# A sliding-window attention and gated MLP kernel on one core: from scheduled and woven tiles to one hand-written order

## The chip, the cores and the metric

The kernel runs on one core of a Trainium2 chip. Times are device microseconds (us) of the whole program. Every ratio uses runs in the normal ("fast") state of the program, on the same chip and in the same rounds as runs of the kernel before; differences in us between two variants can be between sessions. The engines are PE (matmul; PEld is its weight load), DVE (vector), ACT (scalar), POOL (general purpose) and SP (which here only issues DMA). Each engine works off its own queue of instructions in order, and waits for the others where it needs their results.

Words used below: **T** is a tile of 512 tokens (nine of them); **s1** is the first matmul of the MLP for a tile (64 matmuls of 512 columns, in 16 blocks of 4), **s2** the second (another 64). A **bank** is a piece of PSUM of 512 float32 a partition, into which PE writes; both kernels use eight. **Stage 0** is the stretch from s1 of tile 0 to the start of s1 of tile 1.

## The reference

```python
def _attn_ref(q, k, v):                    # q, k, v: [8, 8, 576, 64] float32
    scores = (1 / sqrt(64)) * q @ k^T      # per batch and head
    mask: 0 <= i - j < 64                  # causal, window of 64
    attn = softmax(where(mask, scores, -1e9))
    return attn @ v

def reference(...):
    x = attn_out.transpose(0, 2, 1, 3).reshape(4608, 512)
    h = x @ w_in                           # [512, 2048]
    g = h * clip(h + 3, 0, 6) / 6
    return g @ w_out                       # [2048, 512] -> [4608, 512]
```

## The kernel before

A scheduler (the framework's) reorders instructions. The program text weaves s1 of tile T with s2 of tile T-1, and both with the attention of batch T+1:

```python
    for T in range(NTB):
        side = []
        if T + 1 < B:
            nb = Batch(T + 1)
            if T + 1 < NPE:                           # NPE = 2: batches 0 and 1
                for h0 in (0, 4):
                    nb.cast_qk(pend, 0, h0, 4, pcopy)     # q on POOL
                    nb.cast_qk(pend, 1, h0, 4, vcopy)     # k on DVE
                    ...
            else:
                nb.by_dma(pend)                       # casts, then DMA transposes of q and k
            ...
            side = attention(nb)
        main = zipped(s1(T), s2(T - 1) if T else None)
        weave(main, 32 if T else 16, side, (0.6, 0.5)[T] if T < 2 else 0.0)
```

s1 has two banks (`ps_h`, "hT"), the scores four, the value product one ("o"), s2 one ("acc"). A block of s1 holds its bank until ACT and DVE are done with it:

```python
        for fc in range(NFC):                         # 16 blocks
            hT = ps_h.tile([P, TB], F32, name="hT")
            for g in range(NG):                       # 4 matmuls of 512 columns
                nc.tensor.matmul(hT[:], lhsT=win16[:, g, fc * P : (fc + 1) * P],
                    rhs=xT[:, g, t0 : t0 + TB], start=(g == 0), stop=(g == NG - 1))
            t1 = t1pool.tile([P, TB], BF16, name="t1")
            nc.scalar.activation(out=t1[:], in_=hT[:], func=RELU, bias=half[:], scale=1.0 / 6.0)
            nc.vector.scalar_tensor_tensor(out=gT[:, fc, :], in0=t1[:], scalar=1.0, in1=hT[:], op0=MIN, op1=MULT)
            yield
```

The attention output `opg` (tokens on partitions) must be transposed into `xT`. For batches 0 and 1 PE does it (`xt_pe`), for the others a DMA (`xt_dma`):

```python
    def xt_dma(bt, g):
        opg = opgs.pop((bt.b, g))
        nc.sync.dma_start_transpose(
            out=xT[:, g, bt.b * S : bt.b * S + SP].rearrange("d (k s) -> d k s", s=P),
            in_=opg[:].rearrange("p k h d -> p (k h d)"))
```

The results of s2 leave through two SBUF buffers (`osb`): ACT copies a bank into one of them, and SP issues the store.

The softmax here doesn't subtract the row's maximum and nothing guards it: scores larger than these inputs give would overflow.

## Time and profile before

Times: 374.21 us, median of 3 runs (372.58 to 378.02).

| stretch of the span | what goes on | PE busy of 10 us |
|---|---|---|
| 20 to 50 us | end of batch 0, first loads of w_in | 2.7, 1.9, 6.4 |
| 70 to 90 us | batch 1, first matmuls of s2 | 5.2, 8.4, at a clock of 0.64 and 0.51 |
| 120 to 130 us | batch 2's x, first use of transposes by DMA | 5.9, at a clock of 0.70 |
| 140 us to the end | middle stages and end | 217 of 231 us |

From the page of the kernel before: the span and the busy time of each engine with its share, and, from the span in 40 equal slices, the busy tenths of PE, the granted PE clock in tenths and the busy tenths of the DMA engines.

```profile
span 371.4 us, 5615 instructions
PE 314.0 (85%) x2124; PEld 155.2 (42%) x2160; DVE 187.5 (50%) x342; ACT 183.5 (49%) x293; POOL 71.4 (19%) x104
...
PE   1730499669998699989998997999999999999985
...
PEclk9999999956999699999999999999999999999999
DMA  7999999999119997999899899995112300110111
```

A slice is 9.3 us. From the fifteenth on PE is busy nearly all the time. Before that there are holes, and after two of them the clock is low, so that work in those slices takes up to twice as long. The same from the table by stretches (stretch, its length, busy us and number of instructions of each engine, granted clock, DMA share, GB/s):

```profile
20.00:30.00 10.00, 2.73 (x32) 1.89 (x30) 1.84 (x3) 2.60 (x5) 3.99 (x7) 1.00 1.20 234
30.00:40.00 10.00, 1.89 (x23) 1.57 (x23) 3.64 (x8) 0.64 (x1) 0.99 (x1) 1.00 1.18 246
40.00:50.00 10.00, 6.38 (x47) 4.14 (x49) 3.54 (x10) 2.17 (x4) 4.04 (x5) 1.00 1.14 219
70.00:80.00 10.00, 5.17 (x50) 3.22 (x50) 7.15 (x13) 3.53 (x6) 2.44 (x2) 0.64 0.98 198
80.00:90.00 10.00, 8.40 (x45) 4.26 (x47) 2.75 (x6) 2.66 (x4) 4.02 (x8) 0.51 1.00 192
120.00:130.00 10.00, 5.88 (x30) 2.10 (x31) 1.33 (x2) 2.48 (x5) 1.03 (x2) 0.70 1.15 228
```

A clock of 1.00 is not shown for 20 to 50 us: the clock record of this trace begins at 48.91 us, and a stretch without a record counts as 1.00.

The table of waits gives, for PE, who waited for whom (us in total, times, longest). Three of its lines:

```profile
PE hT L335 <- DVE opg L319: 11.8, 3, 10.6
PE hT L379 <- DMA xT<-opg: 9.2, 6, 2.7
...
PE acc L395 <- ACT osb L402: 3.0, 4, 0.9
```

The longest single wait is 10.6 us on DVE. The timeline (start, duration, engine, line, what it writes and reads, idle time before it and what ended it) shows why DVE was late:

```profile
34.18 0.69 DVE L227 CAST kn<-kst 128x1024 bf16<-128x1024 f32 x1 [8.92 <-DMA kst<-in_k_dram]
34.79 1.15 DVE L292 TENSOR_TENSOR pT_139<-pT_139,mask 128x1920 bf16<-128x1920 bf16 x1
35.86 0.19 DVE L316 RECIPROCAL rec<-o 128x5 f32<-128x5 f32 x1
36.08 0.49 DVE L319 TENSOR_TENSOR opg<-o,rec 128x320 bf16<-128x320 f32 x1
...
36.63 0.50 PE L335 MATMUL hT<-ident,opg 128*128 128x128 bf16 x3 [10.64 <-DVE opg L319]
...
47.16 1.06 PE L379 MATMUL hT<-xT,win_154 128*128 128x512 bf16 x2 [0.22 <-issue]
```

A cast for **batch 1** stood in DVE's queue before batch 0's last mask and normalisation, and waited 8.9 us for a load. PE stood behind it, and the first matmul with w_in came at 47.16 us.

### The profile page before, as it was taken

How to read it: one execution, taken by the hardware profiler on the slowest of the kernel's cores; microseconds unless marked ns; L12 is line 12 of the kernel's file. 1: busy time of each engine (PE TensorE's matmuls, PEld its weight loads, DVE VectorE, ACT ScalarE, POOL GpSimd, SP SyncE). 2: the span in 40 equal slices, each digit the busy share in tenths (PEclk: the TensorE clock that was granted, in tenths of full speed). 3: DMA queues.
4: the chain of work that ended last, by engine and by line, in shares of the span. 5: the costliest groups of instructions: out<-in, count | busy, mean ns of one | idle time of the engine just before them, and what ended most of it. 6: DMA issues, size and time to landing. Idle time of an engine off the chain costs nothing.

```text
span 371.4 us, 5615 instructions
## 1 busy us (share of the span) xinstructions
PE 314.0 (85%) x2124; PEld 155.2 (42%) x2160; DVE 187.5 (50%) x342; ACT 183.5 (49%) x293; POOL 71.4 (19%) x104
## 2 busy tenths in 40 slices
PE   1730499669998699989998997999999999999985
PEld 1520344343444244544544453445444444444432
DVE  6622446842477165646646662766476443433300
ACT  1540158713585266476646564664756354544411
POOL 4523224405200152044204402330000000000000
PEclk9999999956999699999999999999999999999999
DMA  7999999999119997999899899995112300110111
GB/s 225 214 231 239 229 208 194 202 188 193 51 35 180 230 212 122 189 233 213 160 209 221 154 183 210 217 191 116 48 46 49 92 30 28 51 36 29 56 56 58
DMA packets 155867, 54.12 MB, mean 146 GB/s; under 512 B 144064, under 2 KB 150208, under 8 KB 155840
## 3 DMA queue, kind: packets, MB, share of 16 engines
q1 hardware_dynamic: 152640, 49.56, 68.0%
q0 software_dynamic: 3200, 4.19, 6.4%
q8 instruction: 17, 0.28, 0.3%
q14 instruction: 10, 0.08, 0.1%
HBM read 36.70 MB, written 9.44 MB: 124 GB/s over the span
## 4 chain that ended last, share of the span: by engine, by line
PE 69%; DMA 10%; SPq 9%; DVE 5%; ACT 4%; issue 2%; another core or an unknown queue 1%; ACTq 0%; DVEq 0%
PE hT L379 31%; PE acc L395 30%; DMA xT<-opg 6%; SPq L80 4%; DMA kst<-in_k_dram 4%; PE st L276 3%; SPq L105 3%; PE o L305 2%; PE o L310 2%; DVE gT L385 1%; DVE opg L319 1%; SPq L218 1%; DVE pT_136 L292 1%; SPq L111 1%
## 5 line engine op out<-in xcount | busy, mean ns | idle before, releaser
L379 PE MATMUL hT<-xT,win_154 128*128 128x512 bf16 x560 | 151.7, 386 | 13.9 <-DMA xT<-opg 9.2
L395 PE MATMUL acc<-wout_155,gT 128*128 128x512 bf16 x556 | 147.3, 385 | 4.2 <-ACT osb L402 3.0
L379 PEld LDWEIGHTS <-win_154 128*128 128x128 bf16 x576 | 54.9, 99 | 71.0 <-issue 13.5
L395 PEld LDWEIGHTS <-gT 128*128 128x128 bf16 x576 | 53.4, 99 | 67.9 <-issue 10.8
L217 POOL CAST qn<-qst 128x512 bf16<-128x512 f32 (+1 forms) x30 | 19.0, 675 | 104.9 <-DMA qst<-in_q_dram 97.5
L319 DVE TENSOR_TENSOR opg<-o,rec 128x320 bf16<-128x320 f32 x64 | 31.4, 491 | 2.0
L402 ACT COPY osb<-acc 128x512 f32<-128x512 f32 x36 | 21.1, 587 | 20.8 <-PE acc L395 16.9
L316 DVE RECIPROCAL rec<-o 128x5 f32<-128x5 f32 x64 | 12.3, 192 | 27.8 <-PE o L310 27.8
L217 POOL CAST kn<-kst 128x512 bf16<-128x512 f32 (+1 forms) x30 | 17.1, 612 | 19.3 <-DMA kst<-in_k_dram 17.9
L204 POOL CAST V_142<-vst 64x512 bf16<-64x512 f32 (+2 forms) x11 | 11.7, 1082 | 20.4 <-DMA vst<-in_v_dram 16.5
L284 ACT ACTIVATE pT_130<-st 128x768 bf16<-128x768 f32 x16 | 12.2, 810 | 6.8 <-PE st L276 6.8
L292 DVE TENSOR_TENSOR pT_130<-pT_130,mask 128x1920 bf16<-128x1920 bf16 x8 | 10.5, 1312 | 8.0 <-ACT pT_130 L289 8.0
L284 ACT ACTIVATE pT_139<-st 128x768 bf16<-128x768 f32 x16 | 12.1, 807 | 4.4 <-PE st L276 4.2
L292 DVE TENSOR_TENSOR pT_136<-pT_136,mask 128x1920 bf16<-128x1920 bf16 x8 | 10.8, 1349 | 5.5 <-ACT pT_136 L289 5.5
L284 ACT ACTIVATE pT_136<-st 128x768 bf16<-128x768 f32 x16 | 12.0, 807 | 2.2 <-PE st L276 2.2
L284 ACT ACTIVATE pT_133<-st 128x768 bf16<-128x768 f32 x16 | 12.1, 809 | 1.0 <-PE st L276 0.9
L204 POOL CAST V_145<-vst 64x512 bf16<-64x512 f32 (+1 forms) x8 | 10.3, 1312 | 11.7 <-DMA vst<-in_v_dram 11.7
L276 PE MATMUL st<-QT_126,KT_128 64*128 64x192 bf16 (+1 forms) x160 | 10.7, 246 | 1.9 <-DMA KT_128<-kn 1.9
L335 PE MATMUL hT<-ident,opg 128*128 128x128 bf16 x15 | 2.1, 309 | 11.8 <-DVE opg L319 11.8
L292 DVE TENSOR_TENSOR pT_139<-pT_139,mask 128x1920 bf16<-128x1920 bf16 x8 | 9.2, 1154 | 4.9 <-ACT pT_139 L289 4.9
L276 PE MATMUL st<-QT_122,KT_124 64*128 64x192 bf16 (+1 forms) x160 | 10.8, 269 | 1.0 <-ACT KT_124 L256 1.0
L335 PEld LDWEIGHTS <-opg 128*128 128x128 bf16 x40 | 3.4, 130 | 19.5 <-DVE opg L319 19.5
(377 smaller groups left out, 395.7 us busy)
## 6 DMA issues: line engine op xcount, KB each, us to landing
out_dram<-osb SPq DMA_DIRECT2D x36, 256.0 KB, 2.2
qst<-in_q_dram SPq DMA_DIRECT2D x28, 256.0 KB, 4.6
kst<-in_k_dram SPq DMA_DIRECT2D x28, 256.0 KB, 5.2
vst<-in_v_dram SPq DMA_DIRECT2D x28, 256.0 KB, 5.5
vst<-in_v_dram SPq DMA_DIRECT2D x16, 128.0 KB, 6.1
win_154<-in_moe_w_in_dram POOLq DMA_DIRECT2D x4, 512.0 KB, 8.7
wout_155<-in_moe_w_out_dram POOLq DMA_DIRECT2D x4, 512.0 KB, 10.9
qst<-in_q_dram SPq DMA_DIRECT2D x2, 512.0 KB, 10.8
```

The lines of the kernel that those rows point to most:

```text
L80: out.append(nc.sync.dma_start(out=vst[:, 0 : KB - 1, h, :], in_=v[b, h, 0:SM, :].rearrange("(k p) d -> p k d", p=P),))
L105: ins.append(nc.sync.dma_start(out=dst[:, h0 : h0 + heads, :], in_=src[b, h0 : h0 + heads, 0:SM, :].rearrange("h (p j) d -> p h (j d)", j= ...
L204: copy(out=self.V[:kp, k0:k1, h0:h1, 0:D], in_=vst[:kp, k0:k1, h0:h1, :])
L217: pcopy(out=o_ap, in_=i_ap)
L276: nc.tensor.matmul(st[:, h, u, off : off + w], lhsT=bt.KT[h * D : (h + 1) * D, g, kb * P : (kb + 1) * P], rhs=bt.QT[h * D : (h + 1) * D, g ...
L284: nc.scalar.activation(out=pT[:, :, 2 * u : 2 * u + 2, 0:QW], in_=st[:, :, u, 0 : 2 * QW].rearrange("p h (k w) -> p h k w", k=2), func=EXP ...
L292: nc.vector.tensor_tensor(out=pT[:, :, :, 0:QW], in0=pT[:, :, :, 0:QW], in1=mask[:].rearrange("p (h k) w -> p h k w", h=2), op=MULT,)
L316: nc.vector.reciprocal(out=rec[:].unsqueeze(2), in_=ov[:, :, D:VW])
L319: nc.vector.tensor_tensor(out=opgs[bt.b, g][:, :, h, :], in0=ov[:, :, 0:D], in1=rec[:].unsqueeze(2).to_broadcast([P, KB, D]), op=MULT,)
L379: nc.tensor.matmul(hT[:], lhsT=win16[:, g, fc * P : (fc + 1) * P], rhs=xT[:, g, t0 : t0 + TB], start=(g == 0), stop=(g == NG - 1),)
L395: nc.tensor.matmul(acc[:], lhsT=gT[:, fc, ts * P : (ts + 1) * P], rhs=wout16[:, fc, :], start=(fc == 0), stop=(fc == NFC - 1),)
L402: nc.scalar.copy(out=osb[:], in_=acc[:])
```

## The change

The intent: no scheduler; every engine's order is the program text (`manual_schedule`). s1 of a tile runs alone and gets six banks (four in rotation, and two more for blocks 12 and 13), so that ACT and DVE have time to release each. s2 of the **same** tile is woven with the next batch's attention. All batches bring `opg` into `xT` through PE. Loads are held back by explicit rules so that what is needed first has the DMA engines to itself: w_in right behind batch 0, then batch 1's q and k, then w_out, then batch 1's v, then batch 2. The diff is about 660 lines; its core, with cuts marked:

```diff
-    NPE = 2
+    NPE = 3
...
+    ctx.enter_context(tc.manual_schedule())
...
-    def xt_dma(bt, g):
...
+    def s1_bank(fc):
+        if fc in (12, 13):
+            return (ps_o, ps_acc)[fc - 12].tile([P, 512], F32, name=("o", "acc")[fc - 12])[:]
+        if fc % 4 < 2:
+            return h_bank()[:]
+        return ps_st.tile([P, 2, 512], F32, name=f"st{fc % 2}")[:, 0, :] if fc < 12 else h_bank()[:]
...
         for fc in range(NFC):
-            hT = ps_h.tile([P, TB], F32, name="hT")
+            hT = s1_bank(fc)
...
+    w_in = [load_w_in(0, 512, 0, NG)]               # on POOL, between the casts of batch 0's v
+    bt.cast_v(vst0, 0, KB - 1, 4, 6, pcopy)
+    w_in += [load_w_in(512, 1024, 0, NG)]
...
+    st1, ins = load_qk_for_pe(1, 4)
+    for x in ins:
+        after(x, w_in[2], "the weights go first")   # rule 1
+    vst1, insv = load_v_by_head(1)
+    run(s1(0))
...
+    for x in insv:
+        after(x, w_out[2], "the weights go first")  # rule 2
...
+    st2, ins = load_qk_for_pe(2, 4)
+    for x in ins:
+        after(x, w_out[-1], "the weights go first") # rule 3
...
+    def stage_(T, bt, pieces1, pieces2):
+        m = s1(T)
+        for i in range(NFC):
+            run(m, 1)
+            for f in pieces1.get(i, ()):
+                f()
+        m = s2(T, BY_BLOCK)
+        for i in range(16):
+            run(m, 1)
+            for f in pieces2.get(i, ()):
+                f()
...
+            p1 = {13: [f(SS, 0)]}                   # SS scores, N_ value product, X_ transpose into xT
+        p2 = {
+            0: [f(SS, 1)], 3: [f(N_, 0), f(SS, 2)], 5: [f(X_, 0)], 6: [f(N_, 1), f(SS, 3)],
+            8: [f(X_, 1)], 9: [f(N_, 2)], 11: [f(X_, 2)], 12: [f(N_, 3)], 14: [f(X_, 3)],
+        }
...
-        main = zipped(s1(T), s2(T - 1) if T else None)
-        weave(main, 32 if T else 16, side, (0.6, 0.5)[T] if T < 2 else 0.0)
```

All casts of q and k are now on POOL. The number of matmuls with w_in and w_out is the same.

## The prediction

> **What bounds the kernel now.** Three stretches:
>
> (a) Start. In the busy table by stretches PE is busy 2.7, 1.9 and 6.4 of 10 us in 20-30, 30-40 and 40-50 us. The timeline shows the first w_in matmul only at 47.2 us: batch 0's last value products wait behind batch 1's casts (the vector queue held a cast of k for a late load; "hT <- opg" waited 10.6 us in the table of waits), while all loads share the DMA engines (share 1.1-1.2).
>
> (b) 70-90 and 120-130 us: granted clock 0.64, 0.51 and 0.70; in 120-130 PE is busy 5.9 of 10 us.
>
> (c) From 130 us PE is the limit. The chain of waits is about 60% the two large matmuls, four in 0.86 us, so 0.216 us each; 1152 are 249 us. This agrees with the Trainium skill, "TensorE: Matmul & The Clock Gate", section "Back-to-back issue gap" (about 216 ns for 512 columns). Stages last 32 to 35 us, in which the chain spends 2.6-4.5 us on the DMA transpose of xT, but only 9.2 us of PE idle in all are put to it.
>
> **What changes, costed.** Per middle stage: 128 x 0.216 = 27.7 us; scores and value products about 4.8 us (four times 0.5 and eight times 0.35 us, timeline). New: 20 PE transposes of opg, about 0.08 us each, 1.4 us, and four ACT copies of 0.64 us. Six PSUM banks let ReLU (0.69 us) and multiply (0.69 us) run beside PE, whose step is 0.86 us. Walking the new order, in-order stalls come to about 0.8 us. Sum about 34.7 us: the middle gives 0 to 4 us in total.
>
> The gain is at the start. q and k (2.4 MB at about 230 GB/s), then v, then w_in alone: the queue table gives the weights 6.4% of the span for both, so about 12 us for w_in. Estimates: batch 0 ends and s1(0) starts near 23 us, ends near 38; q and k of batch 1 land near 42, w_out near 55, v near 60; stage 0 ends near 70-72 us, with s2(0) done. Before reached the comparable point 25-30 us later. Part is given back by a low clock in the waits of stage 0: the same page, Part 1, says an idle window of about 3.4 us halves the clock; the trace's 0.51 agrees. I allow 4 us. Stage 1 has batch 2's 36 PE transposes and contention for two banks: 34.7 + 2.6 + 3.5 us.
>
> **Sum.** 71 + 4 (clock) + 41 (stage 1) + 5 x 34.7 + 2 x 27.7 + 3 (last copy and store) = 348 us of span, about 350 us of time.
>
> Predicted 350 us, 80% range 339 to 362. Chances: faster by over 2% 0.90, within 2% 0.08, slower 0.02.
>
> **What would show each step.** First w_in matmul at 20-28 us instead of 47. Stage 0's last s2 matmul at 66-78 us. No wait of PE on a DMA of xT; PE over 95% busy from about 115 us; middle stages 34-35.5 us; the last two near 27.7 us each. Low clock, if any, only before 90 us. PE busy total about as before, the span 20-28 us less.
>
> **What would make it wrong.** Strict load order leaving DMA gaps, or POOL, which now does every cast and issues the weights, delaying w_out, so that stage 0 ends after 80 us. Strict order making PE wait at the s1-to-s2 seam (ReLU behind exponentials) or at the two-bank pool by over 1 us a stage. DMA transposes of q and k late, blocking the output stores behind them. A low clock lasting into stage 1. If all go well, 340 us.

## The result, and the profile after

The changed kernel took 344.49 us (median of 4 runs), against 373.53 us for the kernel before in the same session (median of 4). Three of the four runs were fast, 343.76 to 344.62 us. The ratio of the fast runs is 0.9194 (95% interval 0.9100 to 0.9289). A ratio here is the mean time of one kernel's fast runs over that of the other's of the same rounds, so it is not quite the ratio of the quoted medians.

The fourth run, which was the profiled one, took 1241.45 us. From its page, the span and its costliest group (line, engine, operation, shapes, number, then busy us, mean ns of one, and idle time before):

```profile
span 1239.5 us, 5936 instructions
...
L384 PE MATMUL hT<-xT,win 128*128 128x512 bf16 x288 | 275.0, 1213 | 0.2 <-DVE gT L390 0.2
```

PE was busy 99% of that span, and all of its matmuls were slow: five of them in a row took about 4.2 us in the timeline, so about 0.84 us each, against 0.216 us normally. ACT's and DVE's instructions had their usual lengths. The trace of this run holds no clock record. The same program gave seven fast runs besides (three here, four below), so I take it for a state of the chip and not of the kernel; nothing below rests on it, and its cause stays open. A repeat of the unaltered changed kernel gave the trace used here.

**The changed kernel again**

> The changed kernel unaltered, to get a trace of a normal run (its first profile had PE matmuls of about 1.2 us, a slow state that three other runs did not show). All theories: 343 to 346 us. Theory A (the gain is at the start: batch 0 and s1(0) earlier, s2(0) done before stage 1): first w_in matmul at 20 to 28 us, last s2(0) matmul at 66 to 78 us, middle stages 34 to 35.5 us. Rival B (the gain is in the middle: no DMA transposes of xT, six banks): middle stages 31 to 32 us, the start at most 10 us earlier than before.

Measured: 342.61 us (341.59 to 343.38, 4 runs) against 373.60 us; ratio 0.9162 (0.9108 to 0.9217). Its page, the lines that answer to those of before:

```profile
span 339.6 us, 5936 instructions
...
PE 313.2 (92%) x2316; PEld 161.4 (48%) x2316; DVE 195.1 (57%) x339; ACT 202.6 (60%) x324; POOL 84.9 (25%) x108
...
PE   2979899287799999999999999999999999999995
...
PEclk9969999789999999999999999999999999999999
DMA  7999999769968599759976996799500010011011
```

PE's busy time is what it was (313.2 us against 314.0). What is gone is idle time, and nearly all of it was in the first third. One hole is left at slice 8 (59 to 68 us), with a low clock in it and in the next. (The clock record of this trace begins at 16.05 us. It has 0.50 from 19.46 to 26.29 us, in the end of batch 0 and the first matmuls of s1(0), and from 63.84 to 70.66 us.) In the table by stretches:

```profile
20.00:30.00 10.00, 9.23 (x68) 5.37 (x66) 5.93 (x14) 4.78 (x8) 0.65 (x1) 0.69 1.10 198
30.00:40.00 10.00, 9.37 (x45) 4.14 (x43) 7.99 (x12) 8.06 (x12) 6.40 (x8) 1.00 1.11 256
40.00:50.00 10.00, 8.90 (x87) 5.29 (x87) 5.68 (x8) 6.73 (x13) 1.22 (x2) 1.00 1.15 182
...
60.00:70.00 10.00, 3.66 (x32) 2.00 (x30) 1.55 (x5) 1.13 (x2) 3.78 (x5) 0.69 0.61 179
70.00:80.00 10.00, 7.67 (x66) 4.48 (x64) 5.38 (x11) 6.42 (x10) 0.61 (x1) 0.97 0.71 158
80.00:90.00 10.00, 7.54 (x50) 4.03 (x50) 5.35 (x10) 5.85 (x10) 2.95 (x3) 1.00 1.19 214
```

PE's waits:

```profile
PE hT L320 <- ACT xT L351: 6.7, 2, 6.3
PE hT L258 <- POOL qn L228: 5.9, 1, 5.9
PE hT L258 <- DVE gT L390: 3.7, 6, 1.3
...
PE hT L384 <- DVE gT L390: 1.3, 1, 1.3
```

No line names a DMA. The 5.9 us are the first load and cast of the program, before which PE has nothing to do (the kernel before has the same wait, 6.0 us). The largest avoidable wait, 6.3 us, is on an ACT copy. The timeline shows what that copy stood behind, and where s1 begins:

```profile
24.46 0.63 PE L384 MATMUL hT<-xT,win 128*128 128x512 bf16 x1
...
59.03 8.42 SPq L410 DMA_DIRECT2D out_dram<-osb  x3
...
66.50 0.58 ACT L408 COPY osb<-o 128x512 f32<-128x512 f32 x1 [12.47 <-DMA out_dram<-osb]
66.98 0.65 ACT L351 COPY xT<-hT 128x576 bf16<-128x576 bf16 x1
67.68 0.27 PE L320 MATMUL hT<-V,pT 128*128 128x65 bf16 x2 [6.34 <-ACT xT L351]
```

The first matmul with w_in starts at 24.46 us and not at 47.16. At 59.03 us SP begins to issue the first output stores, right after issuing the last of batch 2's 2.4 MB of q and k loads (57.02 to 58.92 us). In the chain of waits that store takes 7.4 us; the page's median for such a store is 2.1. Its SBUF buffer is one of two, so ACT waited 12.5 us to copy the third result, the copy into `xT` stood behind that in ACT's queue, its bank was not released, and PE waited.

In the middle, PE does not wait at all. The first matmul of s1 of tiles 3, 4 and 5 in the timeline:

```profile
146.94 1.24 PE L384 MATMUL hT<-xT,win 128*128 128x512 bf16 x5
...
180.28 1.03 PE L384 MATMUL hT<-xT,win 128*128 128x512 bf16 x4
...
213.61 1.24 PE L384 MATMUL hT<-xT,win 128*128 128x512 bf16 x5
```

The stages are 33.3 us long. In the kernel before, the same mark (first s1 matmul after the last wait for `xT`) is at 161.93, 196.29, 231.34 and 263.45 us: 33.8 us on average.

**Where the 31.8 us of span went.** Count the weight loads of the two large matmuls, which both traces have complete (576 and 576). By 140 us the kernel before had made 156 + 89 = 245 of them, the changed one 192 + 168 = 360. That is 115 matmuls, at 0.216 us each 24.8 us of PE work done sooner; with a score group and some value products that it is also ahead, some 26 us. The remaining 6 us are gained after 140 us: 3.0 us are the waits at the end of the kernel before, which are gone because s2 now alternates between two banks, and the stage marks above give about 0.5 us for each of five middle stages. So four fifths of the gain is in the start. Part of it is clock: from 48.91 us on the records have 23.9 us at half clock in the kernel before and 6.8 us in the changed one. What that is worth was not taken apart.

### The profile page after: what moved, and what is told of

Same layout as the page of the kernel before. It is cut to its first block, busy times and chain, and to the rows that moved or that the text cites. A ratio compares the mean times of both kernels' runs of the same rounds, so it can differ in the third digit from the quotient of the medians.

```text
span 1239.5 us, 5936 instructions
## 1 busy us (share of the span) xinstructions
PE 1229.1 (99%) x2316; PEld 422.8 (34%) x2316; DVE 193.8 (16%) x339; ACT 209.0 (17%) x324; POOL 72.4 (6%) x108
## 4 chain that ended last, share of the span: by engine, by line
PE 99%; DMA 0%; ACT 0%; issue 0%; DVE 0%; POOL 0%; POOLq 0%; ACTq 0%
PE hT L384 21%; PE acc L402 20%; PE o L402 20%; PE st L384 16%; PE st L285 4%; PE hT L346 3%; PE hT L320 3%; PE acc L384 3%; PE o L384 3%; PE hT L258 2%; PE hT L325 2%; PE acc L320 0%; PE o L320 0%; DMA qst<-in_q_dram 0%; PE o L325 0%; PE acc L325 0%
## 5 line engine op out<-in xcount | busy, mean ns | idle before, releaser
L384 PE MATMUL hT<-xT,win 128*128 128x512 bf16 x288 | 275.0, 1213 | 0.2 <-DVE gT L390 0.2
L402 PE MATMUL acc<-wout,gT 128*128 128x512 bf16 x288 | 264.5, 1165 | 0.0
L384 PEld LDWEIGHTS <-win 128*128 128x128 bf16 x576 | 136.3, 238 | 372.3 <-issue 372.0
L402 PE MATMUL o<-wout,gT 128*128 128x512 bf16 x288 | 261.7, 1161 | 0.0
L402 PEld LDWEIGHTS <-gT 128*128 128x128 bf16 x576 | 124.3, 222 | 299.6 <-issue 298.2
L384 PE MATMUL st<-xT,win 128*128 128x512 bf16 x216 | 209.8, 1230 | 0.0
L294 ACT ACTIVATE pT<-st 128x768 bf16<-128x768 f32 x64 | 51.3, 810 | 109.4 <-PE st L285 108.8
L320 PEld LDWEIGHTS <-pT 128*128 128x128 bf16 x320 | 57.0, 196 | 37.0 <-issue 35.9
L389 ACT ACTIVATE t<-st,half 128x512 bf16<-128x512 f32 x54 | 37.1, 687 | 162.9 <-PE st L384 162.9
L390 DVE SCALAR_TENSOR_TENSOR gT<-t,st 128x512 bf16<-128x512 bf16 x54 | 37.1, 688 | 168.6 <-ACT t L389 168.6
L320 PE MATMUL hT<-V,pT 128*128 128x65 bf16 x280 | 62.6, 362 | 0.0
L325 PE MATMUL hT<-V,pT 128*128 128x65 bf16 x224 | 58.0, 361 | 0.0
L285 PE MATMUL st<-QT,KT 64*128 64x192 bf16 (+1 forms) x320 | 55.3, 583 | 0.0
L325 PEld LDWEIGHTS <-pT 128*128 128x128 bf16 x256 | 45.7, 190 | 0.0
```

Source lines behind the costliest of these rows:

```text
L285: nc.tensor.matmul(st[:, h, off : off + w], lhsT=bt.KT[h * D : (h + 1) * D, g, kb * P : (kb + 1) * P], rhs=bt.QT[h * D : (h + 1) * D, g, k ...
L294: nc.scalar.activation(out=pT[:, :, 2 * u : 2 * u + 2, 0:QW], in_=st[:, :, 0 : 2 * QW].rearrange("p h (k w) -> p h k w", k=2), func=EXP, s ...
L320: nc.tensor.matmul(ob, lhsT=pT[:, h, qb, 0:P], rhs=V[:, qb, 2 * g + h, :], start=True, stop=(qb == 0),)
L325: nc.tensor.matmul(ob, lhsT=pT[:, h, qb - 1, P : 2 * P], rhs=V[:, qb - 1, 2 * g + h, :], start=False, stop=True,)
L384: nc.tensor.matmul(hT, lhsT=win16[:, g, fc * P : (fc + 1) * P], rhs=xT[:, g, t0 : t0 + TB], start=(g == 0), stop=(g == NG - 1),)
L389: nc.scalar.activation(out=t1[:], in_=hT, func=RELU, bias=half[:], scale=1.0 / 6.0)
```

## The experiments

All times are medians of fast runs; the ratios are to the kernel before in the same rounds. The changed kernel's own ratio is 0.9162.

| run | us | ratio to before |
|---|---|---|
| changed kernel (e0) | 342.61 | 0.9162 |
| before, x transposed on PE (e1) | 372.65 | 0.9971 |
| before, k casts on POOL (e2) | 367.34 | 0.9844 |
| before, text order (e3) | 436.57 | 1.1676 |
| changed, stores of tile 0 from ACT (e4) | 342.72 | 0.9138 |
| e4, and idle banks in stage 1 (e5) | 339.91 | 0.9064 |
| changed, no load rules (e6) | 338.09 | 0.9019 |
| changed, s1 on two banks (e7) | 383.08 | 1.0236 |
| changed, x transposed by DMA (e8) | 357.94 | 0.9565 |
| changed, batch 1 before w_in (e9) | 348.26 | 0.9327 |
| no load rules, idle banks (e10) | 335.06 | 0.8962 |
| rule 1 alone, idle banks (e11) | 335.62 | 0.8973 |

### Parts of the change in the kernel before

**e1, x by PE in the old order.**

```diff
                 if bt.b < NPE:
                     xt_pe(bt, g, acc_tr())
                 else:
-                    xt_dma(bt, g)
+                    xt_pe(bt, g, tr_of(ps_h, "hT"))
```

> The kernel before with opg of batches 2 to 7 transposed on PE into an s1 bank and copied by ACT, instead of by DMA; nothing else. Theory A: 0 to 6 us faster than before (368 to 374 us), as 9.2 us of PE idle on that DMA go but PE gets 24 x 5 transposes (8 us) more. Rival B: 15 us or more faster (under 359 us), as the chain of before has 22 us of it.

Measured: 372.65 us, ratio 0.9971 (0.9913 to 1.0029): the same time. The waits of PE on the transpose by DMA are gone from its trace, and 120 PE transposes are there instead. Although the chain of waits of the kernel before has that DMA as 6% of the span, taking it out alone is worth nothing measurable. Rival B falls for the old order.

**e2, batch 1's k no longer cast on DVE.**

```diff
-                    nb.cast_qk(pend, 1, h0, 4, vcopy)
+                    nb.cast_qk(pend, 1, h0, 4, pcopy)
```

> The kernel before with the two casts of k of batch 1 on POOL and no longer on DVE, where they stood before batch 0's last mask and normalisation; nothing else. Theory A: the 10.6 us wait of PE on opg goes, first w_in matmul at 36 to 41 us and not 47; time 4 to 10 us less than before (364 to 370 us), not the whole 29 us, as the loads of batch 1 and w_in still share the DMA engines. Rival B: within 2 us of before, as the start is made up later.

Measured: 367.34 us, ratio 0.9844 (0.9761 to 0.9927), about 6 us less. One word repairs the misplaced cast. It is a fifth of the gain. The first w_in matmul came at 43.31 us, later than expected (36 to 41): the trace still has PE busy only 1.2 us between 30 and 40 us, and a new wait of 9.1 us for batch 1's cast:

```profile
PE acc L239 <- POOL rn L234: 9.9, 2, 9.1
```

The rest of the gain is not in this part.

**e3, the old text executed as written.**

```diff
+    ctx.enter_context(tc.manual_schedule())
     stage0, ins0 = load_for_pe(0, 2)
```

> The kernel before, its program text kept, but executed in the order in which it is written, as the changed kernel is; nothing else. Rival C (the scheduler's reordering is what cost the time, any order by hand would do): under 362 us. Theory A: between 368 and 385 us, as the old text starts s1 behind the same loads and casts.

Measured: 436.57 us, ratio 1.1676, which is worse than theory A expected (368 to 385 us). Rival C is out by a wide margin: the scheduler was worth 63 us to the old text. The largest wait of PE in its trace (37.1 us in five times):

```profile
PE st L277 <- DMA KT<-kn: 37.1, 5, 7.6
```

The old text puts a batch's score matmuls where its transposes by DMA have not landed, and the scheduler had moved them. The new text issues these transposes one stage ahead. A hand-written order pays only if every piece is put where its operands are ready; turning the scheduler off gives nothing by itself.

### Parts of the change undone

**e7, s1 on two banks.**

```diff
-            hT = s1_bank(fc)
+            hT = h_bank()[:]
```

> The changed kernel with s1 on the two h banks alone, as before, and not on six. A bank is then held by a matmul group (0.86 us), ReLU (0.69), multiply (0.69) and about 0.3 us of hand-over: about 2.55 us for two banks, so about 1.27 us a block instead of 0.86: 0.4 us x 16 x 9 = 59 us more, 390 to 410 us in all. Rival (two banks are enough, as they were before): within 10 us of the changed kernel.

Measured: 383.08 us, ratio 1.0236 (1.0174 to 1.0299): 40 us more than the changed kernel, and slower than the kernel before. Two successive pairs of blocks in a middle stage:

```profile
159.97 1.89 PE L384 MATMUL hT<-xT,win 128*128 128x512 bf16 x8 [0.64 <-DVE gT L390]
162.49 1.89 PE L384 MATMUL hT<-xT,win 128*128 128x512 bf16 x8 [0.64 <-DVE gT L390]
```

A pair takes 2.52 us, so a block takes 1.26 us, as expected (1.27). The whole was over-estimated (59 us expected), because the first pair of a stage finds its banks free and the seam to s2 hides a part: a middle stage took 38.3 us (157.44 to 195.74 us) instead of 33.3, 5.0 us more and not 6.4. In the kernel before, blocks of s1 and s2 alternate (0.86 us each from 90 to 98 us), which fills the gaps of two banks. s1 alone needs more than two; whether four would do was not tried.

**e8, x by DMA in the new order.**

```diff
     def X_(bt, g):
-        xt_pe(bt, g, h_tr())()
+        if bt.b < NPE:
+            xt_pe(bt, g, h_tr())()
+            return
+        opg = opgs.pop((bt.b, g))
+        nc.sync.dma_start_transpose(out=xT[:, g, ...], in_=opg[:]...)
```

> The changed kernel with opg of batches 3 to 7 transposed by DMA into xT, as before, and not on PE. s1 of the next tile starts right behind the last of these. Theory A: PE waits 2 to 5 us for the last one at each of five stages and saves 1.4 us of transposes, so 5 to 18 us slower than the changed kernel. Rival B (the PE transposes only cost): up to 7 us faster.

Measured: 357.94 us, ratio 0.9565 (0.9505 to 0.9626), about 15 us slower than the changed kernel, inside the range. Two lines of PE's waits:

```profile
PE hT L384 <- DMA xT<-opg: 9.6, 7, 2.3
...
PE hT L384 <- DVE opg L336: 4.0, 4, 2.1
```

These waits come to 13.6 us, while 100 PE transposes were saved (at 0.056 us, worked out below, 5.6 us), so they are not the whole loss. The clock is lower too: the record has four stretches of 3.41 us at 0.50 from 151.97 us on, each behind such waits, where the changed kernel has none. At half pace these cost at most 6.8 us, so my estimate from these traces is 13.6 - 5.6 + 6.8 = 14.8 us, close to the 15; the parts were not measured apart. The result fits e1. With s2 of the previous tile at hand, PE has other work while the DMA runs. With s2 of the same tile, s1 starts right behind the last `opg`, and the DMA's transpose is waited for and PE's is not.

**e9, batch 1 loaded before w_in.**

```diff
+    st1, ins = load_qk_for_pe(1, 4)
+    vst1, insv = load_v_by_head(1)
     w_in = [load_w_in(0, 512, 0, NG)]
+    after(w_in[0], insv[-2], "batch 1 goes first")
...
-    st1, ins = load_qk_for_pe(1, 4)
-    for x in ins:
-        after(x, w_in[2], "the weights go first")
-    vst1, insv = load_v_by_head(1)
```

(Rule 2 is taken out as well, and w_in is issued behind all casts of batch 0's v.)

> The changed kernel with batch 1's q, k and v loaded before w_in and not after it; all of PE's order kept. Theory A (the time at which s1(0) can start is what the start gains): batch 1 is 3.5 MB, about 17 us of loads, the first w_in matmul comes at 38 to 46 us instead of 24, and the time is 8 to 16 us more than the changed kernel's. Rival E (all loads of the first 70 us are needed anyway, order does not count): within 3 us.

Measured: 348.26 us, ratio 0.9327 (0.9283 to 0.9372), about 6 us slower than the changed kernel; both theories expected otherwise (8 to 16, or under 3). PE's wait for w_in is there:

```profile
PE hT L384 <- DMA win<-in_moe_w_in_dram: 12.7, 1, 12.7
```

s1(0) starts at 36.90 us, 12.4 us later than in the changed kernel, but s1 of tile 2 only 6.0 us later (119.48 against 113.45 us). In exchange the 6.3 us of waiting behind the stores are gone (0.4 us in this trace). So an early s1(0) is part of the gain. What a microsecond of it is worth stays open: against the changed kernel it is about half a microsecond, but the edit also takes out rules 1 and 2, and the rules themselves cost time (e6, below). Against e6 (s1(0) at 26.60 us, another session) e9 starts s1(0) 10.3 us later and takes 10.2 us more.

### The hole that is left in the start

**e4, tile 0's stores issued from ACT.**

```diff
-                nc.sync.dma_start(out=out[u0 : u0 + P, :], in_=osb[:])
+                (nc.sync if T else nc.scalar).dma_start(out=out[u0 : u0 + P, :], in_=osb[:])
```

> The changed kernel with the four output stores of tile 0 issued from the ACT queue and not from SP, where they stand behind batch 2's 2.4 MB of q and k loads. In the changed kernel's trace one such store took 7.4 us to land, ACT waited 12.5 us for its buffer (two in all) and PE 6.3 us behind ACT (61 to 68 us), and the clock was low afterwards. Theory D (the backlog of loads behind which the store lies is the cause): the wait of PE falls under 2 us, the time is 4 to 9 us less than the changed kernel's 343 (334 to 339 us). Rival (the DMA engines are full whatever the queue): no more than 2 us less.

Measured: 342.72 us, ratio 0.9138 (0.9089 to 0.9187): no gain over 0.9162 that these intervals show. The rival was right: the stores from ACT still took 6.3 us to land (median of four). SP was free to go on, so batch 2's v was issued from 60.8 us and not from 71.2, and the DMA share stayed at 1.10 and 1.17 from 60 to 70 us, where it had been 1.04 and 0.18. ACT still waited for a store, and PE behind ACT (3.7 us at the longest and not under 2, as theory D expected):

```profile
PE hT L320 <- ACT xT L351: 3.7, 1, 3.7
...
64.00 0.59 ACT L408 COPY osb<-o 128x512 f32<-128x512 f32 x1 [6.45 <-DMA out_dram<-osb]
```

The Trainium skill, "DMA: Bandwidth & Descriptors", section "Issuing engines are not separate DMA queues", says that DMAs of all issuing engines run on the same 16 DMA engines and interleave, and that several issuers only save issue time. This run agrees.

A plainer test would be four `osb` buffers instead of two. It does not build: four need 8 KB a partition, and the build says that 4.125 KB are left in SBUF. That stays untried.

**e5, as e4, with batch 2's transposes in the idle banks of stage 1.** (The definitions of `o_tr` and `acc_tr` are left out; for other batches they give an h bank as before.)

```diff
     def T_(bt, g):
-        later[bt.b, "q", g] = bt.main_t(g, 0, h_tr())
-        later[bt.b, "k", g] = bt.main_t(g, 1, h_tr())
+        later[bt.b, "q", g] = bt.main_t(g, 0, o_tr(bt))      # bank o if bt.b == 2
+        later[bt.b, "k", g] = bt.main_t(g, 1, acc_tr(bt))    # bank acc if bt.b == 2
     def R_(bt):
-        later[bt.b, "r"] = bt.rest_t(h_tr())
+        later[bt.b, "r"] = bt.rest_t(o_tr(bt))
```

> As e4, and in stage 1 the PE transposes of batch 2 go to the two banks that s1 leaves idle there (o and acc) and no longer to its two h banks. In the changed kernel's trace PE waited 5.0 us in stage 1 for the multiply to release an h bank (3.7 us in the transposes, 1.3 us in s1). Theory: those waits go, 3 to 6 us less than e4 (329 to 335 us). Rival: batch 2's q and k now come too late (stage 1 starts 6 us earlier than before) and PE waits for their casts instead, under 2 us gained over e4.

Measured: 339.91 us, ratio 0.9064, which is 2.8 us less than e4 by the medians of the same rounds. The waits for DVE's multiply fell from 5.0 to 1.1 us, so 3.9 us, of which 0.8 us came back as a new wait of s1 for a bank. The gain is just under what was expected (3 to 6 us).

**e6, no load rules.**

```diff
     st1, ins = load_qk_for_pe(1, 4)
-    for x in ins:
-        after(x, w_in[2], "the weights go first")
...
-    for x in insv:
-        after(x, w_out[2], "the weights go first")
...
     st2, ins = load_qk_for_pe(2, 4)
-    for x in ins:
-        after(x, w_out[-1], "the weights go first")
```

> The changed kernel without its three rules that hold loads back (batch 1's q and k until w_in, its v until w_out, batch 2's q and k until w_out); all else kept. Theory A (the order of the loads is part of the gain): w_in shares the DMA engines with batch 1, its s1(0) starts or stalls later, time 3 to 12 us more than the changed kernel's. Rival E (the DMA engines move the same bytes by 70 us either way, the gain is in the order of PE's work): within 2 us.

Measured: 338.09 us, ratio 0.9019 (0.8977 to 0.9062). That is **4.6 us faster** than e4, which was run in the same rounds and equals the changed kernel. Theory A had the sign wrong, and rival E (no difference) was wrong too. In the trace:

```profile
PE hT L384 <- DMA win<-in_moe_w_in_dram: 2.7, 2, 2.1
...
PE hT L320 <- ACT xT L351: 0.4, 1, 0.4
```

Without the rules w_in does come later, and PE waits 2.7 us for it. But the queue of loads never has to wait for a landing before it goes on: batch 2's q and k were issued from 47.5 us and not from 53.1, and by 60 us most of the backlog was gone. The DMA share between 60 and 65 us is 0.21, against 1.04 in the changed kernel. ACT's wait for a store buffer falls to 4.0 us, PE's wait behind it to 0.4 us, and s1 of tile 1 starts at 69.34 us instead of 72.94.

**e10 and e11, both gains together, and rule 1 alone.** e10 is e6 with the edit of banks shown under e5 and the stores back on SP. e11 is e10 with rule 1 put back.

> The changed kernel without its three rules that hold loads back (as e6, 338.1 us) and with batch 2's PE transposes in the two banks that s1 leaves idle in stage 1 (the part of e5 that gained 2.8 us over e4); stores on SP as in the changed kernel. If the two gains are separate, 334 to 337 us; if both removed the same wait, 338 us.

> As e10, but the first rule (batch 1's q and k wait for w_in) kept; the other two dropped. In e6, dropping all three made PE wait 2.7 us for w_in in s1(0), which this rule avoids. Theory F (rules 2 and 3 push batch 2's loads into the first stores, rule 1 is worth its 2.7 us): 1 to 3 us less than e10, first w_in matmul at 24 to 25 us, no wait on w_in, no wait of PE over 2 us behind an ACT copy at 55 to 70 us. Rival G (rule 1 also delays all later loads, so the wait for w_in only moves to the stores): within 1 us of e10 or slower.

Measured, six runs each: e10 335.06 us, ratio 0.8962 (0.8921 to 0.9004); e11 335.62 us, ratio 0.8973 (0.8936 to 0.9011). The two gains add, and e10 is the fastest version, 10% below the kernel before. Rule 1 does not matter for the time (rival G was right): in e11 s1(0) starts at 24.21 us and not at 26.98, and never waits for w_in, but PE then waits 2.8 us for w_out and 2.4 us behind ACT:

```profile
65.06 0.58 ACT L408 COPY osb<-o 128x512 f32<-128x512 f32 x1 [7.58 <-DMA out_dram<-osb]
```

and s1 of tile 1 starts at 70.34 us, against 69.89 in e10. Here the rule that brought w_in forward sent w_out and a store back. It also follows that what the rules cost in e6 lies with rules 2 and 3, which were not taken apart.

## Why the prediction was right or wrong

The prediction was 350 us (339 to 362), and faster with a chance of 0.90. Measured were 344.5 and 342.6 us. The main claim held; here are its terms, with e0's trace.

- **The gain is at the start: right.** The first w_in matmul was predicted at 20 to 28 us and came at 24.46. Stage 0 was to end near 75 us (71, and 4 for the clock); s1 of tile 1 began at 72.94. Some 26 of 31.8 us were gained before 140 us.
- **The cause of the old start: right in part.** e2 shows that the misplaced cast on DVE was worth about 6 us. The rest is in no single part that was tried in the kernel before. e3 shows that it does not come from replacing the scheduler by the written order as such.
- **The loads: sizes pessimistic.** Batch 1's q and k were to land near 42 us; the wait for the last of them ended at 38 us. w_out was to land near 55 us; its third part of four was there by 47.7. PE never waited for w_in or w_out.
- **What stage 0 gives back: right in size, wrong in kind.** The prediction allowed 4 us for a low clock during waits for loads. PE never waited for a load there. The loss was a 6.3 us wait behind an output store, with a clock of 0.50 in 65 to 70 us behind it. The Trainium skill, "TensorE: Matmul & The Clock Gate", Part 1, says that the PE clock halves after an idle window of about 3.4 us. The trace agrees on the half (0.50) but not on the idle time: the clock fell at 63.84 us, 2.5 us after PE stopped, and in the kernel before at 72.81 us, where the wait just before it was 2.3 us. The prediction named stores blocked behind other DMAs, but behind transposes in the middle stages, not behind loads in stage 0.
- **"Strict load order leaving DMA gaps"** was named as what could make it wrong. e6 shows that the strict order cost 4 to 5 us; whether by gaps was not separated.
- **Stage 1: right.** 41 us predicted, 40.5 measured (72.94 to 113.45). The contention for two banks was put at 3.5 us; the waits came to 5.0 us, and e5 got 2.8 us back.
- **Middle stages: the mis-sized term.** 34.7 us predicted, 33.3 measured: five of these are 6.8 us, most of the 8.4 us by which the sum was off (348 against 339.6 us of span). Two parts of it failed, together 1.1 of the 1.4 us a stage. The transposes were put at 0.08 us each, 1.4 us a stage; five of them take 0.28 us from the first to the next matmul (59.77 to 60.05 us in the timeline), so 0.056 each, 1.1 us a stage. And the walk through the queues gave 0.8 us of in-order stalls, where PE is busy 20.00 of every 20 us. "The middle gives 0 to 4 us" held: five stages at 33.8 against 33.3 us give 2.5 us. The 3.0 us at the end of the kernel (two banks for s2) were in no term. The 0.216 us a matmul held in both traces. The section "Back-to-back issue gap" that the prediction names gives about 216 ns as the gap of isolated matmuls and about 131 ns for a sustained stream; these traces, a stream, show 0.216 us.
- **PE busy as before: right** (313.2 against 314.0 us). The span was to fall by 20 to 28 us and fell by 31.8.
- **Last stages 27.7 us each: right** (280.27 to 307.89 us is 27.6).

Why single parts are worth so little alone: the new order of the middle needs more than two banks for s1 (e7: 40 us without) and the transposes on PE (e8: 15 us without), and the transposes gain nothing in the old order (e1; more banks were not tried there). They are the price of running s1 and s2 of the same tile one after the other. What that buys is stage 0: PE has s2(0) to do while batch 1 is still being loaded. That this is the largest part of the start's gain was not tested by itself.

## What to carry to other kernels

Look first at which queue stands in front of the long wait: a single cast for a later batch, in an in-order queue, cost 6 us here, and a store behind a block of loads stopped ACT, and through ACT the PE. A set of parts (bank count, transposes, order) can be worthless one by one and necessary together, so undo them one at a time from the finished version before calling one of them the gain. Test rules that hold loads back by taking them out: here they were written to help and cost 4 to 5 us.

## What the Trainium skill lacked or had wrong

- "DMA: Bandwidth & Descriptors": a figure for how long a store takes behind a backlog of loads would have helped; I found none. Here a 256 KB store took 2.1 us (median) and one behind 2.4 MB of loads 7.4 us; issued from ACT, such stores took 6.3 us (median of four, e4).
- "TensorE: Matmul & The Clock Gate", Part 4, gives about 275 ns for a 128x128 bf16 transpose in a kernel's context. That is near the duration in these traces (231 ns mean), but not what a transpose costs in a dense stream: five took 0.28 us from start to the next matmul, 0.056 us each.
- The same page, Part 1, notes the clock stuck at a quarter for 50 us and more. Here one whole execution of 1239.5 us ran with 512-column matmuls at about 0.84 us each, four times the normal 0.216 us. The run is listed with a clock of 1.00, but its trace holds no clock record at all, so a low clock is neither shown nor ruled out.
- None of the pages that I read says that holding DMA loads back until others have landed can cost more than letting them share the DMA engines: 4 to 5 us here (e6).
